# Where the exp sums are added, and who takes the relu: batch 1 and batch 0 of a fused attention and feed-forward kernel

## The chip, the cores and the metric

The kernel runs on one core of a Trainium2 chip. The metric is the device time of one execution in microseconds (us); the median of three executions counts. The profile is of one further execution. In it PE is TensorE (matmuls), PEld its weight loads, DVE VectorE, ACT ScalarE, POOL GpSimd and SP SyncE.

## What is computed

Attention with an extra term in the softmax's denominator, over 8 batches of 12 heads with 448 tokens and a head size of 64. Its output, put together to 3584 tokens of 768 columns, goes through a feed-forward layer with a squared relu:

```python
def _attn_ref(q, k, v):
    scale = 1.0 / np.sqrt(q.shape[-1])
    scores = scale * np.matmul(q, k.transpose(0, 1, 3, 2))
    m = np.max(scores, axis=-1, keepdims=True)
    e = np.exp(scores - m)
    attn = e / (np.sum(e, axis=-1, keepdims=True) + np.exp(-m) + 1e-09)
    return np.matmul(attn, v).astype(np.float32)

def _moe_ref(x, w_in, w_out):            # x: 3584 x 768, w_in: 768 x 2048, w_out: 2048 x 768
    h = x @ w_in
    r = np.maximum(h, 0.0)
    g = r * r
    return (g @ w_out).astype(np.float32)
```

## The kernel before

The work is cut into units. A unit is a pair of heads of one batch and a range of queries. Units 0 to 5 are the six pairs of batch 0 with queries 0 to 191 (`FIRST` is 192), units 6 to 11 the same pairs with queries 192 to 447, units 12 to 17 the pairs of batch 1 with all 448 queries. From unit 18 on another loop takes three units at a time; the change doesn't touch it.

A unit goes through these steps. `scores` makes two chunks of score matmuls into PSUM tiles `sp`, and ACT takes their exp into `et` in fp16. DVE adds the exps of the four key blocks into `es` (`add_chunks`). `row_sums` adds `es` over the partitions with a matmul against ones, and ACT makes the reciprocal of the sums as Ln and Exp. `values` is the matmul with v, and `normalise` on DVE multiplies its result with the reciprocal into `xt`, the transposed input of the feed-forward layer. Between these, `transposes` brings q and k of a later unit to the layout that the scores need (PE, then a copy on DVE).

The first product of the feed-forward layer is queued in tiles of 512 columns or fewer, each of 12 matmul products (two blocks of features by six blocks of 128 rows, `DCH`), and `drain(ns)` puts some of them, by their nominal time, between the steps of a unit. A tile's last product is followed by a relu and a square on DVE. In this stretch (`COLS2`) each product is two matmuls of 64 columns of weights, side by side in the array.

Each engine has its instructions in the order in which this code makes them. Every PSUM tile of transposes, row sums and first products comes from one pool, `m_psum`, with three buffers.

```python
    m_psum = ctx.enter_context(tc.tile_pool(name="m_psum", bufs=3, space=bass.MemoryType.PSUM))
    ...
    def add_chunks(u, et, es, half, step):
        n = u[3]
        if n == S:
            e = et.rearrange("p (k x) -> p k x", k=RUN)
            if step < 2:
                nc.vector.tensor_add((es, half[:, 0:2 * S])[step], e[:, 2 * step], e[:, 2 * step + 1])
            else:
                nc.vector.tensor_add(es, es, half[:, 0:2 * S])
    ...
    def row_sums(us, sums):
        ...
        zp = mp_tile()
        ...                                   # matmuls of es with ones into zp
        nc.scalar.activation(out=rcp[:, 0:m], in_=zp[:, 0:m], func=AF.Ln, bias=one_b)
        nc.scalar.activation(out=rcp[:, 0:m], in_=rcp[:, 0:m], func=AF.Exp, scale=-1.0)
    ...
    def relu_squared(hp, t0, n, f0, per):
        m = per * n
        rt = r_pool.tile([128, 512], FP16, name="rt")
        nc.vector.tensor_scalar(out=rt[:, 0:m], in0=hp[:, 0:m], scalar1=0.0, scalar2=None, op0=ALU.max)
        r = rt[:, 0:m].rearrange("p (j n) -> p j n", j=per)
        nc.vector.tensor_mul(gs[:, f0:f0 + per, t0 % RING:t0 % RING + n], r, r)
```

The loop over batch 1, `share[0]` being the nominal time of first products that a unit takes in:

```python
    for i in range(2 * NPAIR, 3 * NPAIR):
        ...
        scores(u, et, 0)
        for at in transpose_at.get(i, ()):
            transposes(*at)
        ...
        drain(share[0] * (1.2 if first else 0.45))
        scores(u, et, 1)
        if first:
            ...                               # values and row sums of units 10 and 11
        else:
            done = [prev]
            rcp = row_sums(done, (ess.pop(i - 1)[0:1],))
            values(prev, ets.pop(i - 1), xp)
        drain(share[0] * 0.15)
        for step in range(3):
            add_chunks(u, et, es, half, step)
            drain(share[0] * (0.15, 0.1, 0.15)[step])
        if i == 3 * NPAIR - 1:
            run(ins, len(ins))
            rcps[i] = row_sums([u], (ess.pop(i)[0:1],))
        normalise(done, xp, rcp)
```

In batch 0 the first products start in unit 7. Their first two tiles (features 0 to 511, from the first two of the eight pieces in which `w_in` is loaded) are made early, that is from the pairs that are done: rows of pairs 0 to 3 first, those of pairs 4 and 5 later. At the end of units 1, 3 and 5 a matmul on zeros or two keep TensorE busy (`keep_warm`).

Of the kernel before, what the change touches and what calls it, by code (L numbers as in the profile page):

```python
# [9 lines left out]
FP16 = mybir.dt.float16  # L10
AF = mybir.ActivationFunctionType
ALU = mybir.AluOpType
# [3 lines left out]
def kernel(  # L16
# [9 lines left out]
    nc = tc.nc  # L26

    B, H, S, D = q.shape
    NT, DM = out.shape
    DF = moe_w_in.shape[1]  # L30
    NPAIR = H // 2
    DCH = DM // 128
    NFFB = DF // 128
    RUN = 4
    P = S // RUN
# [17 lines left out]
    z_pool = ctx.enter_context(tc.tile_pool(name="z", bufs=3))  # L53
    r_pool = ctx.enter_context(tc.tile_pool(name="r", bufs=2))
    osb_pool = ctx.enter_context(tc.tile_pool(name="osb", bufs=2))

    s_psum = ctx.enter_context(tc.tile_pool(name="s_psum", bufs=2, space=bass.MemoryType.PSUM))
    x_psum = ctx.enter_context(tc.tile_pool(name="x_psum", bufs=1, space=bass.MemoryType.PSUM))
# [149 lines left out]

    def add_chunks(u, et, es, half, step):
        n = u[3]  # L210
        if n == S:
            e = et.rearrange("p (k x) -> p k x", k=RUN)
            if step < 2:
                nc.vector.tensor_add((es, half[:, 0:2 * S])[step], e[:, 2 * step], e[:, 2 * step + 1])  # L214
            else:
                nc.vector.tensor_add(es, es, half[:, 0:2 * S])  # L216
        elif step == 1:
            nc.vector.tensor_add(half[:, 0:4 * n], et[:, 0:4 * n], et[:, 4 * n:8 * n])
        elif step == 2:
            f = half[:, 0:4 * n].rearrange("p (h j n) -> p h j n", h=2, j=2)  # L220
            nc.vector.tensor_add(es[:, 0:2 * n].rearrange("p (h n) -> p h n", h=2), f[:, :, 0, :], f[:, :, 1, :])
# [48 lines left out]
    def mp_tile(dtype=FP32):  # L270
        if joined[0] >= 0:
            joined[0] += 1
        pool, name = (x_psum, "xp") if joined[0] > 0 and joined[0] % 4 == 0 else (m_psum, "mp")
        return pool.tile([128, 512] if dtype == FP32 else [128, 2, 512], dtype, name=name)
# [2 lines left out]

    FULL, COLS2, ROWS2 = range(3)
    mode = [FULL]
    ots = {}  # L280

    def product(out_, lhsT, rhs, start, stop):
# [7 lines left out]
    def relu_squared(hp, t0, n, f0, per):  # L290
        m = per * n
        rt = r_pool.tile([128, 512], FP16, name="rt")
        nc.vector.tensor_scalar(out=rt[:, 0:m], in0=hp[:, 0:m], scalar1=0.0, scalar2=None, op0=ALU.max)  # L293
        r = rt[:, 0:m].rearrange("p (j n) -> p j n", j=per)
        nc.vector.tensor_mul(gs[:, f0:f0 + per, t0 % RING:t0 % RING + n], r, r)  # L295

# [11 lines left out]
        relu_squared(hp, t0, n, f0, per)  # L308
        yield n / 2.4

    def tiles_in_early(n, f0, per, ready):

        xt = xts[0]
        m = per * n
        hps = [mp_tile(), mp_tile()]
        for t, dcs in ((0, range(ready)), (1, range(ready)), (0, range(ready, DCH)), (1, range(ready, DCH))):
            for j in range(per):
                fb = f0 + per * t + j
                for dc in dcs:
                    product(hps[t][:, j * n:(j + 1) * n], win[:, dc, fb * 128:(fb + 1) * 128],  # L320
                            xt[:, dc, 0:n], start=(dc == 0 and j == 0), stop=(dc == DCH - 1 and j == per - 1))
                    if dc < DCH - 1 or j < per - 1:
                        yield n / 2.4
            if dcs[-1] == DCH - 1:
                relu_squared(hps[t], 0, n, f0 + per * t, per)
                yield n / 2.4
# [68 lines left out]
    ins, outs = [], []  # L395
    groups = [0]

    def queue(t0, n):

        per = max(1, 512 // n)  # L400
        first = 0
        if t0 + n == FIRST:
            first = 2 * per
            ns = first * DCH * n / 2.4
            ins.append([ns, ns, tiles_in_early(n, 0, per, DCH - 2)])
        for f0 in range(first, NFFB, per):
            ns = per * DCH * n / 2.4
            ins.append([ns, ns, tile_in(t0, n, f0, per)])
# [10 lines left out]
    def left():  # L419
        return sum(t[0] for t in ins)  # L420

    def one(tiles):

        got = next(tiles[0][2])
        tiles[0][0] -= got
        if tiles[0][0] < 1.0:
            tiles.pop(0)
        return got

    def drain(ns):  # L430
        while ins and ns > 0:
            ns -= one(ins)

    def run(tiles, n=1):
        for _ in range(min(n, len(tiles))):
            for _ in tiles.pop(0)[2]:
                pass

    FIRST = 192
# [9 lines left out]
    def keep_warm(n):  # L449
        wp = m_psum.tile([128, 512], FP32, name="mp")  # L450
        for _ in range(n):
            nc.tensor.matmul(wp, warm[:, 0:128], warm, start=True, stop=True)

    share = [0.0]
    ets, ess, rcps = {}, {}, {}
# [27 lines left out]
    def values_of(at, xp):  # L483
        values(units[at], ets.pop(at), xp, at % 2 * units[at][3])
# [9 lines left out]
    for i in range(NPAIR):  # L494
        u, et, es, half = begin(i)
        mode[0] = COLS2
        scores(u, et, 0)
        if i < 2:
            scores(u, et, 1)
        if i in (3, 5):  # L500
            rcp = sums_of(i - 3)
        for at in transpose_at.get(i, ()):
            transposes(*at)
        if i == 0:
            cast(0, 2)
            keep_warm(1)
        if i:
            sums(i - 1)
        if i > 1:
            scores(u, et, 1)  # L510
        if i in (2, 4):
            xp = x_psum.tile([128, 512], FP32, name="xp")
        if i in (2, 3, 4):
            values_of(i - 2, xp)
        if i == 4:
            values_of(3, xp)
        if i in (3, 5):
            normalise(units[i - 3:i - 1], xp, rcp)
        if i in (1, 3, 5):
            keep_warm(1 + i // 5)  # L520


    for i in range(NPAIR, 2 * NPAIR):
        u, et, es, half = begin(i)
        two = units[i - 2:i] if i % 2 == 0 else None
        if i % 2 or i == NPAIR:
            xp = x_psum.tile([128, 512], FP32, name="xp")
        mode[0] = COLS2
        scores(u, et, 0)
        if i == NPAIR:  # L530
            sums(i - 1)
            values_of(i - 2, xp)
            values_of(i - 1, xp)
            rcp = sums_of(i - 2)
            normalise(two, xp, rcp)
            scores(u, et, 1)
            queue(0, FIRST)
            share[0] = left() / (NPAIR + 4)
        else:
            for at in transpose_at.get(i, ()):  # L540
                transposes(*at)
            drain(16 * FIRST / 2.4 if i == NPAIR + 1 else share[0] * 0.45)
            scores(u, et, 1)
            values_of(i - 1, xp)
            if two:
                rcp = sums_of(i - 2)
            drain(share[0] * 0.3)
        add_chunks(u, et, es, half, 1)
        if two and i > NPAIR:
            normalise(two, xp, rcp)  # L550
        add_chunks(u, et, es, half, 2)
        if i > NPAIR:
            drain(share[0] * 0.25)
        if i == NPAIR + 5:
            load_natural(2, 0, 3)
            for n0 in (0, HALF):
                for j in range(2):
                    load_wout(n0, j, 2)


    for i in range(2 * NPAIR, 3 * NPAIR):
        u, et, es, half = begin(i)
        prev = units[i - 1]
        first = i == 2 * NPAIR
        if not first:
            xp = x_psum.tile([128, 512], FP32, name="xp")
        mode[0] = COLS2
        scores(u, et, 0)
        for at in transpose_at.get(i, ()):
            transposes(*at)  # L570
        if i == 2 * NPAIR + 3:
            load_natural(2, 3, 6)
            load_v(2, 0, 6)
            stage(3)
# [3 lines that stand above are left out]
            done = units[i - 2:i]  # L578
            values(prev, ets.pop(i - 1), xp, prev[3])
            rcp = row_sums(done, (ess.pop(i - 2)[0:1], ess.pop(i - 1)[0:1]))  # L580
        else:
            done = [prev]
            rcp = row_sums(done, (ess.pop(i - 1)[0:1],))
            values(prev, ets.pop(i - 1), xp)
        drain(share[0] * 0.15)
        for step in range(3):
            add_chunks(u, et, es, half, step)
            drain(share[0] * (0.15, 0.1, 0.15)[step])
        if i == 3 * NPAIR - 1:
            run(ins, len(ins))  # L590
            rcps[i] = row_sums([u], (ess.pop(i)[0:1],))
        normalise(done, xp, rcp)
        if first:
            queue(FIRST, S - FIRST)
            share[0] = left() / (NPAIR - 0.2)
# [103 lines left out]
```

The softmax here doesn't subtract the row's maximum and nothing guards it: scores larger than these inputs give would overflow.

## Time and profile before

| | |
|---|---|
| median of three executions | 412.69 us (412.59 to 413.04) |
| profiled execution | 412.49 us, span of the instructions 410.6 us |
| granted TensorE clock | 0.999 |
| stretch of the changed code | about 17 to 69 us |
| one add of 112x896 fp16 | 0.62 us |
| one exp of 112x896 | 0.915 us |

A profile's page gives busy times over the whole span; since the kernel goes through stages with different limits, the busy times by stretch and the timeline of the stretch that is changed say more. In the timeline a row is an instruction or several of a kind: the start, the length, the engine, the line of the kernel, the tiles it writes and reads, their shape, and in brackets how long the engine had been idle before and what ended that. In the list of waits a row has the waiting engine and line, what it waited for, then the total, how many times, and the longest. Lines that matter here: L189 and L201 are scores, L169 exp, L214, L216, L218 and L221 the adds, L236 values, L250 row sums, L253 and L254 Ln and Exp of the reciprocal, L262 and L265 normalise, L158 transposes, L164 their copy, L286 the first product in this mode, L293 the relu, L295 the square, L352 the second product, L452 the warm matmuls.

### The profile page before, as it was taken

The numbers are of one execution on the slowest core, as the hardware profiler recorded it, in microseconds if no ns is written. First come the engines' busy times: TensorE is split into PE (matmuls) and PEld (weight loads), VectorE is DVE, ScalarE is ACT, GpSimd is POOL, SyncE is SP. The second block draws the span as 40 slices with busy tenths as digits, with TensorE's granted clock in tenths as the row PEclk, the third lists the DMA queues.
The fourth block names the chain that finished last, engine by engine and source line by source line (L and its number), as shares of the span: only waits on it lengthen the run. The fifth ranks groups of instructions, "written<-read, shape, count | busy, mean of one in ns | idle before, by whom it ended". The sixth has DMA issues, their size and how long they took to land.

```text
span 410.6 us, 10685 instructions
## 1 busy us (share of the span) xinstructions
PE 401.0 (98%) x4715; PEld 259.0 (63%) x4715; DVE 289.8 (71%) x554; ACT 234.4 (57%) x312; POOL 36.3 (9%) x58
## 2 busy tenths in 40 slices
PE   7899998999999999999999999999999999999997
PEld 3577676755576666666566666667566665555664
DVE  3778896978976787777876788867876789186000
ACT  5998997667393745559383755739464663100111
POOL 7524030020000200001000030001000000000000
PEclk9999999999999999999999999999999999999999
DMA  9999999689114891499304992297102010010222
GB/s 203 197 198 197 203 202 219 127 132 219 60 42 107 135 219 25 98 183 182 100 2 114 168 179 64 77 188 124 41 2 69 11 41 2 38 40 0 78 77 78
DMA packets 75823, 45.58 MB, mean 111 GB/s; under 512 B 42560, under 2 KB 72000, under 8 KB 75456
## 3 DMA queue, kind: packets, MB, share of 16 engines
q0 software_dynamic: 28848, 22.16, 35.6%
q1 hardware_dynamic: 46208, 22.05, 23.1%
q8 instruction: 37, 0.61, 0.6%
q10 hardware_dynamic: 720, 0.69, 0.5%
q14 instruction: 10, 0.08, 0.1%
HBM read 45.69 MB, written 17.93 MB: 155 GB/s over the span
## 4 chain that ended last, share of the span: by engine, by line
PE 89%; ACT 4%; DVE 4%; DMA 1%; issue 1%
PE mp L286 24%; PE mp L352 17%; PE mp L288 11%; PE xp L286 8%; PE sp L201 6%; PE xp L352 5%; PE mp L236 5%; PE xp L288 3%; PE xp L236 3%; PE sp L189 3%; ACT et L169 3%; PE mp L250 2%; PE mp L158 1%; DMA et<-in_k_dram 1%; DVE qk L164 1%; ACT rcp L253 1%
## 5 line engine op out<-in xcount | busy, mean ns | idle before, releaser
L169 ACT ACTIVATE et<-sp 112x896 f16<-112x896 f32 (+2 forms) x144 | 125.2, 915 | 40.7 <-PE sp L201 30.6
L352 PE MATMUL mp<-wout,gs 64*128 64x384 f16 x896 | 115.2, 322 | 0.0
L286 PEld LDWEIGHTS <-win 128*64 128x64 f16 x1536 | 83.9, 110 | 45.6 <-issue 1.5
L286 PE MATMUL mp<-xt,win 128*64 128x448 f16 (+2 forms) x1200 | 107.0, 323 | 0.3 <-DVE qk L164 0.2
L293 DVE TENSOR_SCALAR rt<-mp 128x448 f16<-128x448 f32 (+2 forms) x96 | 59.7, 622 | 26.3 <-PE mp L286 13.8
L352 PEld LDWEIGHTS <-gs 64*128 64x128 f16 x1152 | 58.1, 94 | 21.1
L295 DVE TENSOR_TENSOR gs<-rt 128x448 f16<-128x448 f16 (+2 forms) x128 | 50.2, 392 | 4.4
L352 PE MATMUL xp<-wout,gs 64*128 64x384 f16 x256 | 53.1, 323 | 0.0
L253 ACT ACTIVATE rcp<-mp,one_b 128x448 f32<-128x448 f32 (+2 forms) x42 | 26.5, 630 | 41.9 <-PE mp L250 41.7
L361 ACT ACTIVATE ot<-mp 128x384 f32<-128x384 f32 (+1 forms) x16 | 7.6, 477 | 64.5 <-PE mp L288 48.2
L201 PE MATMUL sp<-qk 64*112 64x224 f16 x480 | 43.1, 258 | 0.0
L169 ACT ACTIVATE nn<-sp 112x896 f16<-112x896 f32 x48 | 41.7, 917 | 1.6
L201 PEld LDWEIGHTS <-qk 64*112 64x112 f16 x480 | 30.6, 128 | 14.2 <-issue 3.6
L286 PE MATMUL xp<-xt,win 128*64 128x448 f16 x336 | 36.5, 352 | 0.0
L288 PEld LDWEIGHTS <-gs 128*128 128x128 f16 x256 | 24.4, 98 | 15.1 <-issue 0.4
L236 PEld LDWEIGHTS <-vn 112*64 112x64 f16 x432 | 22.4, 109 | 15.4 <-issue 3.9
L288 PE MATMUL mp<-wout,gs 128*128 128x384 f16 (+1 forms) x192 | 30.3, 317 | 0.0
L214 DVE TENSOR_TENSOR es<-et 112x896 f16<-112x896 f16 x30 | 18.7, 623 | 15.8 <-ACT et L169 15.3
L254 ACT ACTIVATE rcp<-rcp 128x448 f32<-128x448 f32 (+2 forms) x48 | 27.7, 577 | 1.5
L189 PE MATMUL sp<-qk 64*112 64x448 f16 (+2 forms) x192 | 25.8, 320 | 1.4 <-ACT et L169 0.6
L216 DVE TENSOR_TENSOR es<-es,half 112x896 f16<-112x896 f16 x42 | 26.2, 623 | 1.0
L293 DVE TENSOR_SCALAR rt<-xp 128x448 f16<-128x448 f32 x32 | 19.9, 622 | 8.2 <-PE xp L286 6.7
(63 smaller groups left out, 340.0 us busy)
## 6 DMA issues: line engine op xcount, KB each, us to landing
vn<-in_v_dram POOLq DMA_DIRECT2D x7, 672.0 KB, 9.0
out_dram<-ot SPq DMA_DIRECT2D x9, 384.0 KB, 2.3
win<-in_moe_w_in_dram POOLq DMA_DIRECT2D x8, 384.0 KB, 14.2
wout<-in_moe_w_out_dram POOLq DMA_DIRECT2D x4, 768.0 KB, 18.0
stage_q<-in_q_dram POOLq DMA_DIRECT2D x4, 676.0 KB, 11.3
stage_k<-in_k_dram POOLq DMA_DIRECT2D x4, 676.0 KB, 14.7
out_dram<-ot SPq DMA_DIRECT2D x8, 288.0 KB, 9.0
out_dram<-ot SPq DMA_DIRECT2D x9, 192.0 KB, 2.7
```

The lines of the kernel that those rows point to most:

```text
L169: nc.scalar.activation(out=out_, in_=in_, func=AF.Exp, scale=scale)
L189: nc.tensor.matmul(sp[:, h, o:o + n], qk[r, 1, x + P * kk:x + P * kk + P], qk[r, 0, x + q0:x + q0 + n], start=True, stop=True)
L201: nc.tensor.matmul(sp[:, odd, h * (S // 2):(h + 1) * (S // 2)], qk[r, which, kx:kx + 2 * P - 1:2], qk[r, 0, x:x + S // 2], start=True, sto ...
L216: nc.vector.tensor_add(es, es, half[:, 0:2 * S])
L236: nc.tensor.matmul(xp[64 * h:64 * h + 64, o:o + n], vns[b][:, 2 * pr + h, kk, :], of_head(chunk(et, u, kk // 2, kk), u, h), start=(kk == 0 ...
L253: nc.scalar.activation(out=rcp[:, 0:m], in_=zp[:, 0:m], func=AF.Ln, bias=one_b)
L254: nc.scalar.activation(out=rcp[:, 0:m], in_=rcp[:, 0:m], func=AF.Exp, scale=-1.0)
L286: nc.tensor.matmul(out_[x:x + 64], lhsT[:, x:x + 64], rhs, start=start, stop=stop)
L288: nc.tensor.matmul(out_, lhsT, rhs, start=start, stop=stop)
L293: nc.vector.tensor_scalar(out=rt[:, 0:m], in0=hp[:, 0:m], scalar1=0.0, scalar2=None, op0=ALU.max)
L295: nc.vector.tensor_mul(gs[:, f0:f0 + per, t0 % RING:t0 % RING + n], r, r)
L352: nc.tensor.matmul(o[:, 0:w], g[x:x + 64], wout[x:x + 64, fb, n0:n0 + w], start=(fb == 0), stop=(fb == NFFB - 1))
```

## The change

In batch 1 the three adds of a unit (exps of blocks 0 and 1, of 2 and 3, and the two sums) become two: one add twice as wide, of both halves of `et` into a tile of its own, and one that adds the halves of that. They move from the unit itself to the next unit, after the first chunk of its scores. The last unit keeps the three adds, the second and third now after all that is left of the first products. In units 13, 15 and 17 one relu goes to ScalarE. Both are meant to take load and interruptions off VectorE, which the relus of the first product need in the same stretch.

In batch 0 the first two tiles of the first product start in unit 5, where the warm matmuls stood, with the rows of pairs 0 and 1 alone; rows of pairs 2 and 3, and then 4 and 5, follow in unit 7 and 8. It is meant to give TensorE useful work in place of the zeros and to leave less for later. The shares of first products that go between a unit's steps are distributed anew, odd units of batch 0 taking more of them ahead of the second scores.

```diff
     def add_chunks(u, et, es, half, step):
         n = u[3]
-        if n == S:
+        if step == 3:
+            h = wide.tile([P, RUN * S], FP16, name="wide")
+            nc.vector.tensor_add(h, et[:, 0:RUN * S], et[:, RUN * S:2 * RUN * S])
+            nc.vector.tensor_add(es, h[:, 0:2 * S], h[:, 2 * S:4 * S])
+        elif n == S:
...
     def relu_squared(hp, t0, n, f0, per):
         m = per * n
         rt = r_pool.tile([128, 512], FP16, name="rt")
-        nc.vector.tensor_scalar(out=rt[:, 0:m], in0=hp[:, 0:m], scalar1=0.0, scalar2=None, op0=ALU.max)
+        if relus[0]:
+            relus[0] -= 1
+            nc.scalar.activation(out=rt[:, 0:m], in_=hp[:, 0:m], func=AF.Relu)
+        else:
+            nc.vector.tensor_scalar(out=rt[:, 0:m], in0=hp[:, 0:m], scalar1=0.0, scalar2=None, op0=ALU.max)
...
-    def tiles_in_early(n, f0, per, ready):
+    def tiles_in_early(n, f0, per):
...
-        for t, dcs in ((0, range(ready)), (1, range(ready)), (0, range(ready, DCH)), (1, range(ready, DCH))):
+        steps = (range(0, 2), range(2, DCH - 2), range(DCH - 2, DCH))
+        for t, dcs in [(t, dcs) for dcs in steps for t in range(2)]:
...
-        if i in (1, 3, 5):
-            keep_warm(1 + i // 5)
+        if i in (1, 3):
+            keep_warm(1)
+        if i == 5:
+            queue(0, FIRST)
+            drain(8 * FIRST / 2.4)
...                                            (units 6 to 11)
-            queue(0, FIRST)
-            share[0] = left() / (NPAIR + 4)
+            share[0] = left() / (NPAIR + 3.5)
         else:
             for at in transpose_at.get(i, ()):
                 transposes(*at)
-            drain(16 * FIRST / 2.4 if i == NPAIR + 1 else share[0] * 0.45)
+            drain(12 * FIRST / 2.4 if i == NPAIR + 1 else share[0] * (0.45 if two else 0.7))
             scores(u, et, 1)
             values_of(i - 1, xp)
+            drain(share[0] * (0.3 if two else 0.1))
             if two:
                 rcp = sums_of(i - 2)
-            drain(share[0] * 0.3)
...
-            drain(share[0] * 0.25)
+            drain(share[0] * (0.25 if two else 0.2))
...                                            (units 12 to 17)
+        final = i == 3 * NPAIR - 1
         scores(u, et, 0)
+        if not first:
+            add_chunks(prev, ets[i - 1], *ess[i - 1], 3)
...
-        drain(share[0] * 0.15)
-        for step in range(3):
-            add_chunks(u, et, es, half, step)
-            drain(share[0] * (0.15, 0.1, 0.15)[step])
-        if i == 3 * NPAIR - 1:
+        relus[0] = int(i in (13, 15, 17))
+        drain(share[0] * 0.3)
+        if final:
+            add_chunks(u, et, es, half, 0)
+        drain(share[0] * 0.25)
+        relus[0] = 0
+        if final:
             run(ins, len(ins))
+            add_chunks(u, et, es, half, 1)
+            add_chunks(u, et, es, half, 2)
             rcps[i] = row_sums([u], (ess.pop(i)[0:1],))
         normalise(done, xp, rcp)
```

## The prediction

> **What bounds the kernel now.** I read the page first, then busy time by stretch, then TensorE's waits between 17 and 69 us, where all the changed code runs, and last the timelines of that stretch.
>
> The page's busy line:
>
> ```profile
> PE 401.0 (98%) x4715; PEld 259.0 (63%) x4715; DVE 289.8 (71%) x554; ACT 234.4 (57%) x312; POOL 36.3 (9%) x58
> ```
>
> The busy times by stretch (stretch and its length, then busy us of PE, PEld, DVE, ACT and POOL with the number of instructions in brackets, clock, DMA):
>
> ```profile
> 17.00:36.00 19.00, 17.16 (x304) 12.73 (x304) 14.27 (x30) 17.03 (x22) 5.98 (x8) 1.00 1.45 197
> 36.00:45.00 9.00, 8.40 (x136) 5.96 (x134) 8.12 (x18) 8.63 (x12) 3.19 (x4) 1.00 1.44 199
> 45.00:60.00 15.00, 14.79 (x230) 10.78 (x226) 13.67 (x26) 13.48 (x19) 3.51 (x5) 1.00 1.32 204
> 60.00:70.00 10.00, 8.54 (x128) 6.07 (x128) 7.55 (x14) 7.18 (x11) 0.00 (x0) 1.00 1.37 219
> ```
>
> After 70 us TensorE (PE) is busy to within some 1%, so whatever the first 70 us lose or gain moves the end one for one. Within them no engine has room: from 45 to 60 us PE is at 99%, VectorE (DVE) at 91%, ScalarE (ACT) at 90%. TensorE's waits from 17 to 69 us (total us, times, longest):
>
> ```profile
> PE xp L236 <- DVE xt L265: 1.3, 2, 0.9
> PE mp L250 <- DVE es L216: 1.1, 1, 1.1
> PE sp L189 <- ACT et L169: 0.6, 2, 0.4
> PE mp L286 <- DVE qk L164: 0.2, 1, 0.2
> PE mp L250 <- DVE qk L164: 0.2, 1, 0.2
> ```
>
> They and four small ones give under 4 us: the most a perfect change could return is 1%. The timeline around the sums of unit 14 (start, length, then what):
>
> ```profile
> 50.38 0.62 DVE L214 TENSOR_TENSOR half<-et 112x896 f16<-112x896 f16 x1
> 51.03 0.62 DVE L216 TENSOR_TENSOR es<-es,half 112x896 f16<-112x896 f16 x1
> 51.58 0.62 DVE L262 TENSOR_TENSOR xt<-xp,rcp 128x448 f16<-128x448 f32 x1
> 52.11 0.61 DVE L164 COPY qk<-mp 128x896 f16<-128x896 f16 x1
> 52.78 0.38 PE L250 MATMUL mp<-es,ones 112*64 112x448 f16 x2 [0.20 <-DVE qk L164]
> ```
>
> Two things are to be seen. DVE works in program order: adds of unit 14, normalise of 13, copy of the new transposes. And PE's row sums, which need a PSUM buffer of the pool "mp" (three), waited not for their input `es`, ready at 51.65, but for that copy: they got the buffer which the transposes had used. The pool reuses the buffer freed longest ago, and this explains the other such waits too.
>
> [...] an add of 1024 columns took 0.69 us, of 512 columns 0.42, so 0.53 ns a column and 0.15 us fixed. [...]
>
> **The change part by part.**
>
> *Adds.* Of a unit's three adds (starts 0.54, 0.65 and 0.55 us apart, 1.74 together) the first two become one of 1792 columns, by the slope 0.15 + 1792 x 0.53 ns = 1.10 us, and 0.55 follows: 1.67. DVE saves 0.07 us a unit: nothing. What counts is the new place. Before, unit 14's adds ran as soon as its exps ended. Now they stand at the start of unit 15, *behind* the normalise of unit 13, which needs the reciprocal (ACT, Ln and Exp) that comes after unit 14's exps. And the copy of the transposes, for whose buffer the row sums wait, stands behind the adds. From the end of a unit's exps the chain is: Ln and Exp 1.14, normalise 0.59, adds 1.13 + 0.55, copy 0.62, semaphore 0.05: 4.1 us. The row sums of unit 15, at 57.59 today, would come 4.1 us after 54.14 (end of its exps), at 58.2: late by 0.6 even when nothing else is late.
>
> *Relus on ACT.* By the column counts a relu of 128x512 costs ACT about what its Ln of 512 columns costs, 0.69 us; DVE saves 0.71 in three units. But it queues behind the unit's Ln and Exp, and the square, still on DVE, stands before the normalise, so DVE now waits for ACT just there: about 1 us more in the chain above.
>
> *Unit by unit.* I count products per slice of the code (share now about 1945 ns) and step from one unit's row sums to the next with the measured lengths. Before, these stood at 42.88, 47.69, 52.78, 57.59, 63.19 and 67.21 us (units 12 to 17).
> - Unit 12: reciprocal 40.9, normalise to 41.5, adds to 43.2, copy to 43.8: 43.9, late by 1.0.
> - Unit 13: relu on ACT to 46.0, square, normalise 46.4, adds 46.9 to 48.6, copy to 49.2: 49.25, late by 1.55.
> - Unit 14: values 0.97 and 6 products 0.65 after the row sums, relu and square 1.06, normalise 0.55, adds 1.65, copy 0.65: 5.6 us on, 54.85, late by 2.1.
> - Unit 15: relu on ACT after 10 products, 57.0 to 57.65, square, normalise, adds: 60.4, late by 2.8 (the buffer here is the relu's, not the copy's).
> - Unit 16: the relu behind 2 products, normalise 62.7, adds from 63.25, two copies from 64.9; the tile of first products needs the buffer of the first copy, so PE stops at 63.8 until 65.55, and unit 16's second scores come behind that: 66.85, late by 3.65.
> - Unit 17: here the second and third add are put after all remaining products, so behind ACT's relu (69.45 to 70.1), a square, the first add, the last relu (from 71.05) and its square: adds from 72.1, row sums at 73.4 instead of 67.21. Even without earlier delay this order costs over 1 us: today the last relu comes after the adds.
>
> Sum: 1.0 + 0.55 + 0.5 + 0.7 + 0.85 + 2.55 = 6.2 us.
>
> *Batch 0.* Eight first products replace two warm matmuls of 0.54 us. They need `win`'s pieces 0 and 1 (columns up to 511). GpSimd's queue shows when those land, for its later loads wait for them (timeline, 17 to 21 us):
>
> ```profile
> 17.30 0.82 POOL L105 DMA_DIRECT2D win<-in_moe_w_in_dram  x1 [1.85 <-DMA win<-in_moe_w_in_dram]
> ...
> 18.98 0.85 PE L236 MATMUL xp<-et,vn 112*64 112x192 f16 x16 [0.86 <-DVE xt L265]
> ...
> 19.30 0.82 POOL L105 DMA_DIRECT2D win<-in_moe_w_in_dram  x1 [1.18 <-DMA win<-in_moe_w_in_dram]
> ...
> 20.39 0.58 ACT L253 ACTIVATE rcp<-mp,one_b 128x384 f32<-128x384 f32 x1 [0.43 <-PE mp L250]
> ```
>
> The records of landings put piece 0 at 17.02 and piece 1 at 19.02 us, just ahead of these two issues. So four of the eight products hold PE from 17.5 to 19.05 with unit 6's scores behind them: these come at 19.45 instead of 17.70, the row sums end at about 20.9 instead of 20.35, and ACT, which is gapless from 20.39 to 29.6, starts 0.5 late. What is gained is the later distribution: 3 instead of 6 products after the values of units 9 and 11, eight products fewer to do. From 29.6 us on, where ACT has gaps (0.47, 0.26, 0.63), I find unit 12's scores 0.5 us earlier. Net 0.
>
> Total: 412.7 + 6.2 = 418.9. Of such a chain some slack is usually overlooked, so 418.4.
>
> **Rivals.**
> 1. *DVE relief wins.* DVE loses 3 x 0.71 + 5 x 0.07 = 2.5 us of work, the gaps at 52.78, 61.68 and 67.21 close, and the early products take the wait at 18.98: 409.5. For it: DVE is gapless from 49 to 64 us. Against: its work is not the matter but its order, and PE is dense there anyway.
> 2. *Only the end counts.* If the row sums get another buffer than the copy's, or the adds slip in ahead of the reciprocal's wait, units 12 to 16 keep their 4.8 us and only unit 17's late adds (1.2 to 2.5) stay: 414 to 415. Against: the wait at 52.78.
> 3. *`win` decides.* If the weights land later than in this execution, all of it moves with them, since PE stops in order: up to 2 us on top, 420.5.
>
> **Range and chances.** The sign rests on two separate orders (adds behind the normalise, last adds behind the last relu), so slower is far more likely than faster; the size is a sum of six delays, each good to about 0.4 us, errors mostly in one direction. Range 414.0 to 420.8. Over 2% would be above 420.9: 0.13. Over 2% faster would be below 404.4, more than all waits give: 0.02.
>
> **What would show it.** Right: DVE idles at the squares of units 13 and 15 for ACT's relu and at the normalises for the reciprocal; the largest PE waits are row sums for DVE's copy (units 12 to 14), then for `es`; from 45 to 62 us a unit takes 5.3 to 6 us; row sums of unit 17 near 73; PE waits near 17.5 us for `win`'s landing; wide adds of 1.1 us. Wrong: row sums keep 4.8 us per unit, or DVE's wide add starts right at the end of the exps.

## The result: 422.63 us, 2.4% slower

The changed kernel takes 422.63 us in the median of four runs (421.25 to 423.43), the kernel before 412.72 on the same chip: a ratio of 1.0236, 95% interval 1.0208 to 1.0263. The direction was predicted, the size was not: 9.9 us lost instead of 5.7.

The busy line of the page after (span 421.6 us; 410.6 before) hardly differs from that of before. TensorE shows 4.6 us more, the others 2.4 at most:

```profile
PE 405.6 (96%) x4713; PEld 259.5 (62%) x4713; DVE 287.6 (68%) x546; ACT 236.8 (56%) x315; POOL 36.5 (9%) x58
```

The busy times by stretch of the kernel after, with the columns as before; the one behind POOL is the granted TensorE clock:

```profile
17.00:36.00 19.00, 16.51 (x278) 12.49 (x277) 13.21 (x28) 16.41 (x21) 4.89 (x6) 0.91 1.45 197
36.00:45.00 9.00, 7.90 (x124) 5.61 (x123) 5.60 (x11) 7.55 (x10) 4.29 (x6) 1.00 1.44 199
45.00:60.00 15.00, 12.83 (x192) 9.61 (x192) 10.81 (x20) 12.72 (x19) 3.52 (x5) 1.00 1.32 204
60.00:80.00 20.00, 14.66 (x199) 9.86 (x197) 12.21 (x22) 12.34 (x17) 0.00 (x0) 0.87 0.81 136
```

Two things are to be seen. From 45 to 60 us the three busy engines do less in the same time: TensorE 12.83 us against 14.79, VectorE 10.81 against 13.67, ScalarE 12.72 against 13.48. Nothing became the bound; they wait for each other. And the clock stands at 0.91 and 0.87 in two stretches where it was 1.00 before. TensorE's waits from 17 to 80 us:

```profile
PE mp L256 <- DVE es L222: 3.5, 1, 3.5
PE mp L293 <- DVE qk L166: 2.3, 2, 1.2
PE mp L256 <- DVE qk L166: 2.2, 3, 0.9
PE mp L293 <- DMA win<-in_moe_w_in_dram: 1.3, 1, 1.3
PE mp L256 <- DVE es L216: 0.6, 1, 0.6
```

(L256 is now the row sums, L293 the first product, L166 the copy of the transposes, L216 and L222 the adds.) The waits of before add up to under 4 us, these to over 10. The timeline around the row sums of units 14 and 15, in order of start, shows how they arise:

```profile
57.06 0.38 PE L256 MATMUL mp<-es,ones 112*64 112x448 f16 x2 [0.88 <-DVE qk L166]
...
58.31 0.58 ACT L260 ACTIVATE rcp<-rcp 128x448 f32<-128x448 f32 x1
59.33 0.60 ACT L302 ACTIVATE rt<-mp 128x512 f16<-128x512 f32 x1 [0.44 <-PE mp L293]
...
59.96 0.42 DVE L306 TENSOR_TENSOR gs<-rt 128x512 f16<-128x512 f16 x1 [1.89 <-ACT rt L302]
...
60.30 0.62 DVE L268 TENSOR_TENSOR xt<-xp,rcp 128x448 f16<-128x448 f32 x1
60.84 1.08 DVE L215 TENSOR_TENSOR wide<-et 112x1792 f16<-112x1792 f16 x1
...
61.96 0.62 DVE L216 TENSOR_TENSOR es<-wide 112x896 f16<-112x896 f16 x1
62.50 0.62 DVE L166 COPY qk<-mp 128x896 f16<-128x896 f16 x1
62.63 0.38 PE L256 MATMUL mp<-es,ones 112*64 112x448 f16 x2 [0.64 <-DVE es L216]
```

VectorE stands idle for 1.89 us in front of a square whose relu is on ScalarE. The relu itself waited for TensorE's product, as its bracket says (0.44 us), and not for Ln and Exp, which had ended by 58.89 us. Behind the square, in program order, come the normalise, the wide add (1.08 us) and the second add, and TensorE's row sums wait for the last. At the end of batch 1:

```profile
72.54 0.43 DVE L306 TENSOR_TENSOR gs<-rt 128x512 f16<-128x512 f16 x1 [3.05 <-ACT rt L302]
72.89 0.62 DVE L220 TENSOR_TENSOR es<-et 112x896 f16<-112x896 f16 x1
73.42 0.68 DVE L304 TENSOR_SCALAR rt<-mp 128x512 f16<-128x512 f32 x1
74.14 0.42 DVE L306 TENSOR_TENSOR gs<-rt 128x512 f16<-128x512 f16 x1
74.48 0.62 DVE L220 TENSOR_TENSOR half<-et 112x896 f16<-112x896 f16 x1
75.14 0.62 DVE L222 TENSOR_TENSOR es<-es,half 112x896 f16<-112x896 f16 x1
...
75.81 0.58 PE L256 MATMUL mp<-es,ones 112*64 112x448 f16 x2 [3.46 <-DVE es L222]
...
76.74 1.81 PE L364 MATMUL mp<-wout,gs 64*128 64x384 f16 x10
```

The last row: ten matmuls of the second product take 1.81 us. Before, ten took 1.03:

```profile
67.75 1.03 PE L352 MATMUL mp<-wout,gs 64*128 64x384 f16 x10
```

TensorE runs at half its clock behind this wait of 3.46 us (the windows at the end of this document show 0.50 from 74.71 us on).

The row sums of units 12 to 17 serve as time marks of batch 1. Their starts in the timelines, in us, and what follows the last to the end of the span:

| kernel | unit 12 | 13 | 14 | 15 | 16 | 17 | from there to the end |
|---|---|---|---|---|---|---|---|
| before | 42.88 | 47.69 | 52.78 | 57.59 | 63.19 | 67.21 | 343.4 |
| predicted | 43.9 | 49.25 | 54.85 | 60.4 | 66.85 | 73.4 | 343.4 |
| after | 46.10 | 51.31 | 57.06 | 62.63 | 69.25 | 75.81 | 345.8 |

From unit 12 to 17 the prediction has 29.5 us and the chip took 29.7, against 24.3 before. The two places where it failed are ahead of unit 12 (2.2 us more than predicted) and behind unit 17 (2.4 us more).

### The profile page after: what moved, and what is told of

It is laid out like the page before. It is cut to its first block, busy times and chain, and to the rows that moved or that the text cites. A ratio compares the mean times of both kernels' runs of the same rounds, so it can differ in the third digit from the quotient of the medians.

```text
span 421.6 us, 10673 instructions
## 1 busy us (share of the span) xinstructions
PE 405.6 (96%) x4713; PEld 259.5 (62%) x4713; DVE 287.6 (68%) x546; ACT 236.8 (56%) x315; POOL 36.5 (9%) x58
## 4 chain that ended last, share of the span: by engine, by line
PE 86%; DVE 5%; ACT 3%; DMA 3%; POOL 1%; issue 1%; POOLq 0%
PE mp L293 23%; PE mp L364 18%; PE mp L295 10%; PE xp L293 8%; PE sp L203 6%; PE mp L242 5%; PE xp L364 5%; PE xp L295 3%; PE xp L242 3%; DMA win<-in_moe_w_in_dram 3%; PE sp L191 2%; PE mp L256 2%; ACT et L171 1%; DVE wide L215 1%; ACT rcp L259 1%
## 5 line engine op out<-in xcount | busy, mean ns | idle before, releaser
L364 PE MATMUL mp<-wout,gs 64*128 64x384 f16 x896 | 117.0, 328 | 0.0
L293 PEld LDWEIGHTS <-win 128*64 128x64 f16 x1536 | 84.4, 110 | 49.1 <-issue 3.5
L293 PE MATMUL mp<-xt,win 128*64 128x448 f16 (+2 forms) x1200 | 108.3, 324 | 3.7 <-DVE qk L166 2.3
L304 DVE TENSOR_SCALAR rt<-mp 128x448 f16<-128x448 f32 (+2 forms) x93 | 57.8, 621 | 26.2 <-PE mp L293 13.6
L364 PEld LDWEIGHTS <-gs 64*128 64x128 f16 x1152 | 56.5, 95 | 24.4 <-issue 1.9
L293 PE MATMUL xp<-xt,win 128*64 128x448 f16 x336 | 36.4, 352 | 0.0
L220 DVE TENSOR_TENSOR es<-et 112x896 f16<-112x896 f16 x25 | 15.6, 623 | 17.6 <-ACT et L171 17.2
L222 DVE TENSOR_TENSOR es<-es,half 112x896 f16<-112x896 f16 x37 | 23.1, 623 | 0.9
```

The costliest lines, as they stand in the source:

```text
L293: nc.tensor.matmul(out_[x:x + 64], lhsT[:, x:x + 64], rhs, start=start, stop=stop)
L364: nc.tensor.matmul(o[:, 0:w], g[x:x + 64], wout[x:x + 64, fb, n0:n0 + w], start=(fb == 0), stop=(fb == NFFB - 1))
```

## The experiments

The theory after comparing the two traces had three parts: VectorE's order in batch 1, a loss in batch 0 of some 2 us that I had put at zero, and the clock behind the waits (0.50 for 6.83 us from 74.71 us on, in the trace of after). Every median stands beside that of the kernel before on the same chips, 412.55 to 412.61 us.

**Batch 1 alone, batch 0 alone.** The first kernel has batch 0 as before (`keep_warm` in unit 5, products from unit 7 on, old shares), the second batch 1 as before (three adds in the unit, no relu on ScalarE).

> Only the batch 1 part (wide adds in the next unit, relus on ScalarE, late adds of unit 17); batch 0 as before. Theory (order on VectorE plus half clock after unit 17's wait): row sums of unit 12 about 1 us later than the 42.88 us of before, 29 to 30 us from there to those of unit 17 instead of 24.3, then a clock window or two at half: 419.5 to 421. Rival (batch 0 and its wait for the weights is the main cause): 414 to 416.

> Only the batch 0 part (early tiles in unit 5, new shares); batch 1 as before. Theory: first products wait for the second piece of the weights until 19.2 us, first scores of unit 12 about 2 us later than the 35.87 us of before, and batch 1 hands that on: 414 to 415. Rival 1 (batch 1 alone costs, batch 0 is harmless): 412.7. Rival 2 (batch 0 is the main cause): 418 or more.

Batch 1 alone: 420.98 us, ratio 1.0202 (1.0187 to 1.0218). Row sums of unit 12 at 43.47, of unit 17 at 73.23, then 345.8 to the end. Batch 0 alone: 415.14, ratio 1.0062 (1.0047 to 1.0077), with nothing lost behind unit 17. Batch 1 costs 8.4 us and batch 0 2.5. Batch 1's own row sums are those of the prediction within 0.5 us (unit 12: 43.47 for 43.9; unit 17: 73.23 for 73.4). Batch 0 alone has the row sums of unit 12 at 43.86, 1.0 us late, and loses another 1.1 us in unit 16 (6.69 us for 5.60), where a tile of first products stands ahead of the second scores and waits for the buffer of the copy:

```profile
64.21 0.95 PE L293 MATMUL mp<-xt,win 128*64 128x256 f16 x14 [1.30 <-DVE qk L166]
```

In batch 1 alone the same place has a wait of 1.23 us, and unit 16 takes 6.61. Either part is enough for this loss, which fits that the two losses (8.4 and 2.5) add up to more than the 9.9 of the changed kernel.

**Relus back on VectorE**, all else as changed.

```diff
-        relus[0] = int(i in (13, 15, 17))
+        relus[0] = 0
```

> The changed kernel with all relus on VectorE. Theory: the deferred adds still stand behind the normalise; only the waits of the squares for ScalarE go (about 1 us in units 13, 15 and 17): 419.5 to 420.5. Rival (the relu on ScalarE is the cause): 415 to 417.

421.18 us, ratio 1.0207 (1.0192 to 1.0222): 1.45 us better than the changed kernel, less than expected. Part of that is the clock: executions at the same granted clock differ by 0.5 to 1.1 us (at 0.996, 420.53 and 420.78 for 421.25; at 0.992, 421.58 and 421.79 for 422.61 and 422.66). Between the row sums, unit 17 gained 0.7 us (5.84 for 6.56) and unit 15 nothing (5.67 for 5.57); unit 13 took 6.43 us for 5.21, with a stretch of half clock from 45.1 to 48.5 us in it. The relu is not the main cause.

**One relu each moved to ScalarE in the kernel before.**

> The kernel before with one relu of each of the units 13, 15 and 17 on ScalarE and nothing else (unit 13 has no tile that ends in these slices, so two relus move). Theory (the square waits for ScalarE's Ln and Exp and holds up the adds behind it): row sums of unit 15 and of unit 17 about 1 us later each: 413.8 to 415. Rival (VectorE's relief wins): 411.5 to 412.3.

413.80 us, ratio 1.0035 (1.0022 to 1.0048). Taking these relus off VectorE gained nothing; here is unit 17 (timeline), which took 4.97 us instead of 4.02:

```profile
66.22 0.58 ACT L296 ACTIVATE rt<-mp 128x512 f16<-128x512 f32 x1
66.83 0.43 DVE L300 TENSOR_TENSOR gs<-rt 128x512 f16<-128x512 f16 x1 [2.74 <-ACT rt L296]
67.17 0.62 DVE L214 TENSOR_TENSOR half<-et 112x896 f16<-112x896 f16 x1
67.83 0.62 DVE L216 TENSOR_TENSOR es<-es,half 112x896 f16<-112x896 f16 x1
...
68.50 0.38 PE L250 MATMUL mp<-es,ones 112*64 112x448 f16 x2 [2.08 <-DVE es L216]
```

ScalarE's relu is short (0.58 us), but it comes after Ln and Exp, and the square holds up the last two adds, whose exps were done at 65.2. In unit 15 it cost 0.17 us only, not the 1 us expected.

**Adds back into the unit**, still as a wide add and a second one, between the two slices of first products.

```diff
-        if not first:
-            add_chunks(prev, ets[i - 1], *ess[i - 1], 3)
...
         if final:
             add_chunks(u, et, es, half, 0)
+        else:
+            add_chunks(u, et, es, half, 3)
         drain(share[0] * 0.25)
```

> The changed kernel with the wide add and its second add in the unit itself, between the two slices of first products, instead of the next unit; all else as changed. Theory: row sums come 4.8 to 5.1 us apart again, unit 12 to 16 lose little; the late adds of unit 17 and batch 0 remain: 416 to 418. Rival (the relu on ScalarE or the width of the add is the cause): 420 to 423.

419.95 us, ratio 1.0177 (1.0160 to 1.0193): a miss for the theory as I had worded it. The row sums of units 12 to 17 stand 5.92, 5.76, 4.85, 6.62 and 6.57 us apart (changed kernel: 5.21, 5.75, 5.57, 6.62, 6.56). Unit 15 gained and, against the row sums ahead of it, unit 12; unit 13 lost 0.7. In VectorE's timeline the adds are now ahead of the normalise, but in unit 13 VectorE stands idle for 2.23 us in front of a square that waits for ScalarE's relu, and the adds are behind it:

```profile
46.60 0.36 DVE L306 TENSOR_TENSOR gs<-rt 128x384 f16<-128x384 f16 x1 [2.23 <-ACT rt L302]
46.87 1.08 DVE L215 TENSOR_TENSOR wide<-et 112x1792 f16<-112x1792 f16 x1
47.99 0.62 DVE L216 TENSOR_TENSOR es<-wide 112x896 f16<-112x896 f16 x1
48.53 0.62 DVE L268 TENSOR_TENSOR xt<-xp,rcp 128x448 f16<-128x448 f32 x1
49.07 0.61 DVE L166 COPY qk<-mp 128x896 f16<-128x896 f16 x1
```

From the row sums of units 10 and 11 to those of unit 17 this kernel needs 33.9 us, the changed one 34.9. So the place in the next unit costs 1.0 us there; the rest of the 2.7 us between the medians goes with the clock (all four executions at 0.996, those of the changed kernel at 0.988 to 0.996). What stays, by the timeline, is that all the adds of a unit stand behind a relu and square that wait for products made after the row sums. The row sums of one unit, products, relu, square, both adds, normalise, copy and the row sums of the next unit then form a ring, and swapping adds and normalise in it changes little. Before, the first add at least ran ahead of that relu.

**Unit 17's adds first**, ahead of the last relus, in the changed kernel.

```diff
+        if final:
+            add_chunks(u, et, es, half, 0)
+            add_chunks(u, et, es, half, 1)
+            add_chunks(u, et, es, half, 2)
         relus[0] = int(i in (13, 15, 17))
         drain(share[0] * 0.3)
-        if final:
-            add_chunks(u, et, es, half, 0)
         drain(share[0] * 0.25)
         relus[0] = 0
         if final:
             run(ins, len(ins))
-            add_chunks(u, et, es, half, 1)
-            add_chunks(u, et, es, half, 2)
```

> The changed kernel with all three adds of unit 17 ahead of its last relus, right behind unit 16's values. Theory (the late adds make TensorE idle 3.46 us, and that idle halves the clock for 6.8 us after it): row sums of unit 17 come 3.3 to 3.6 us after those of unit 16 instead of 6.57, no half clock after them, 416.5 to 418. Rival (the half clock comes of all the gaps before, or of something else than the idle time): only the 3 us, 419.5 to 420.

417.70 us (416.71 to 418.20), ratio 1.0115 (1.0098 to 1.0131): 4.9 us of the 9.9 come back. The row sums of unit 17 follow those of unit 16 by 3.02 us (6.57 changed, 4.02 before). The tail, from there to the end, is 343.8 us, with no half clock behind unit 17 (this profile, at a granted clock of 0.996, has a stretch at 0.51 in batch 1, from 46.0 to 49.4 us), and the place of the adds is all that was altered.

**TensorE kept busy in that wait**: 14 matmuls on zeros ahead of unit 17's row sums, nothing else.

```diff
             add_chunks(u, et, es, half, 2)
+            keep_warm(14)
             rcps[i] = row_sums([u], (ess.pop(i)[0:1],))
```

> The changed kernel with 14 warm matmuls (zeros, 14 times 0.21 us) in the wait of unit 17's row sums, nothing else. Theory: the row sums still come about 6.6 us after those of unit 16, but the clock stays full after them; from there to the end 343.4 to 343.8 us instead of 345.8: 420.2 to 421. Rival (the 2.4 us lost behind the wait are another wait, of ScalarE or of buffers): no change, 422.6.

(The 0.21 us agree with the trace of before, where one such matmul takes 0.39 us and two take 0.60.) 419.99 us in the median (419.38 to 423.62), ratio 1.0197 (1.0160 to 1.0233). The row sums still come 6.57 us after those of unit 16, but the tail is 343.4 us as before, and ten matmuls of the second product take 0.98 us:

```profile
71.28 3.19 PE L464 MATMUL mp<-warm 128*128 128x512 f16 x14
74.81 0.38 PE L256 MATMUL mp<-es,ones 112*64 112x448 f16 x2 [0.34 <-DVE es L222]
75.12 0.40 PE L191 MATMUL sp<-qk 64*112 64x448 f16 x2
75.35 0.98 PE L364 MATMUL mp<-wout,gs 64*128 64x384 f16 x10
```

The granted clock from 75.12 to 78.53 us is 1.00. The 2.4 us behind the wait are thus the clock. Useless work of 3 us made the kernel 2.6 us faster. Three runs were at a granted clock of 1.0; the fourth, 423.62, at 0.992. Where its half clock lay was not recorded.

**Batch 0's two suspects undone together**, with batch 1 as before: in unit 5 just the four products of the first tile (`drain(4 * FIRST / 2.4)`, whose weights have landed), and the shares 0.45, 0.3 and 0.25 for odd units too.

> Only the batch 0 part, with its two suspects undone: in unit 5 just the four early products of the first tile (first piece of the weights), and the old shares in odd units. Theory: no wait for the second piece and none of 1.2 us for the copy in front of unit 11's second scores: 412.3 to 413.2. Rival (starting early costs by itself, by buffers that are held longer): 414.5 to 415.2 as with the whole batch 0 part.

414.69 us, ratio 1.0050 (1.0037 to 1.0064): a miss. The wait for the weights was gone, but not the one in unit 11 (timeline of TensorE):

```profile
34.12 0.25 PE L293 MATMUL mp<-xt,win 128*64 128x192 f16 x2
35.81 0.52 PE L293 MATMUL mp<-xt,win 128*64 128x192 f16 x8 [1.44 <-DVE qk L166]
36.26 0.42 PE L191 MATMUL sp<-qk 64*112 64x256 f16 x4
```

A new tile of first products begins ahead of unit 11's second scores, needs the PSUM buffer that VectorE's copy must first empty, and TensorE holds the scores back with it. Batch 0 alone has the same with 1.11 us. It is the tiles' borders that count: in the kernel before a tile ends exactly at the end of that slice and the next begins behind scores and values, when the copy is done:

```profile
33.67 0.58 PE L286 MATMUL mp<-xt,win 128*64 128x192 f16 x10
34.18 0.42 PE L189 MATMUL sp<-qk 64*112 64x256 f16 x4
34.54 0.63 PE L236 MATMUL xp<-et,vn 112*64 112x256 f16 x8
35.25 0.69 PE L286 MATMUL mp<-xt,win 128*64 128x192 f16 x12
```

By the code, 16 products were made up to the end of unit 7's first slice there; here they are 20 (4 and 16), as in batch 0 alone (8 and 12), and the shares differ too (775 and 741 ns for 768). This shifts the border.

**The same early start, with the borders kept**: the kernel before with four early products, and the later shares such that each slice from unit 8 on holds the products of before.

```diff
-            queue(0, FIRST)
-            share[0] = left() / (NPAIR + 4)
+            share[0] = (left() + 4 * FIRST / 2.4) / (NPAIR + 4)
...
-            drain(16 * FIRST / 2.4 if i == NPAIR + 1 else share[0] * 0.45)
+            drain(12 * FIRST / 2.4 if i == NPAIR + 1 else share[0] * 0.45)
```

> The kernel before with four products of the first tile in unit 5 in place of the two warm matmuls, and the later shares set so that from unit 8 on each slice holds the same products as before. Theory (the batch 0 part loses by the place of the tiles' borders: a tile's first product that needs the buffer of unit 11's copy stands in front of the second scores): no wait of 1.2 us there, 412.2 to 412.8. Rival (the early start costs by itself): 414.5.

412.55 us, ratio 1.0000 (0.9992 to 1.0009): the loss is gone and nothing is gained. The early start of four products by itself is harmless and useless. (Unlike the kernel above, it also makes the row sums of batch 0's pairs ahead of a slice of products, as before; no run has that alone.) TensorE does four products fewer in unit 7 and waits for ScalarE instead (its waits for exp 1.1 us in place of 0.6).

**Only the width left** of the batch 1 part: no relu on ScalarE, both adds in the unit, unit 17's adds first. The batch 0 part is still in.

> The changed kernel without relus on ScalarE, with the two adds in the unit itself and unit 17's adds ahead of its last relus: of the batch 1 part only the width of the first add and one block of adds instead of three places are left. Theory (order costs, width doesn't): the loss of the batch 0 part, 2.5 us, and 0.5 to 1 us for adds in one block behind the relu: 415.2 to 416.3. Rival (the wide add itself, or the tile it needs, costs): 417.5 or more.

416.66 us, ratio 1.0098 (1.0084 to 1.0111), 0.4 us over what was expected. Against batch 0 alone it loses 1.5. The row sums: 5.08, 5.76, 4.81, 6.62, 3.02 us apart; batch 0 alone has 5.06, 5.19, 4.81, 6.69, 4.13. So unit 17 gains 1.1, unit 14 loses 0.6 (its adds in one block behind the relu). The rest lies outside batch 1: a lower clock (the profiled runs were granted 0.995 and 0.999), and 0.7 us behind unit 17, where the second product now waits for the last relu. The width itself shows no cost: from start to start 1.12 us for the wide add against 0.54 and 0.65 for the two that it replaces. No run has the wide add alone in the kernel before.

**A version that beats both.** In the kernel before, the wait of 1.1 us for unit 17's sums comes of a relu between its adds. Here the three adds come first:

```diff
+        last = i == 3 * NPAIR - 1
         for step in range(3):
             add_chunks(u, et, es, half, step)
-            drain(share[0] * (0.15, 0.1, 0.15)[step])
+            if not last:
+                drain(share[0] * (0.15, 0.1, 0.15)[step])
```

> The kernel before with all three adds of unit 17 ahead of the relus that follow unit 16's values. Theory (TensorE's wait of 1.1 us for unit 17's sums comes from a relu that stands between its adds): row sums of unit 17 about 3.0 us after those of unit 16 instead of 4.02, 411.5 to 412. Rival (what is gained there is lost in a wait for the last tiles): 412.6.

411.70 us in 11 runs, ratio 0.9979 (0.9970 to 0.9987). The row sums come 3.02 us after unit 16's instead of 4.02; 0.2 of that is lost behind them. Then with two more moves: the four early products with the borders kept, and each normalise of batch 1 behind the copy of the next unit.

> The kernel before with three moves: unit 17's adds first (0.9 us less, as run alone), four early products instead of warm matmuls, and each normalise of batch 1 behind the copy of the next unit's transposes, so that the row sums get their buffer 0.5 us earlier. Theory: the waits at 52.78 and 61.68 us go (0.4 us and less) and little more: 410.8 to 411.5. Rival (normalise later holds up the values, which need its PSUM tile): 412 or more.

411.58 us in 10 runs, ratio 0.9975 (0.9966 to 0.9984): not to be told from the one before, and just over the expected range. The row sums of unit 14 follow those of unit 13 0.27 us sooner, those of unit 15 follow 0.1 later.

## Why the prediction was right and wrong

*Adds and unit 17: right.* 6.2 us were worked out for batch 1. In the changed kernel units 12 to 17 take 29.7 us for 24.3, 5.4 more, and unit 12's adds, first behind the normalise, 1.2 (5.19 us from the row sums of units 10 and 11 instead of 4.02): 6.6. The waits are those that were named: the row sums of units 12 to 14 wait for the copy, those of 15 and 17 for `es`. The late adds of unit 17 count most (4.9 us with the clock behind them), the deferral 1.0 us between the row sums.

*Relus: the words wrong, the steps right.* "About 1 us more in the chain above" did not show in unit 15, which took 5.57 us with its relu on ScalarE and 5.67 without. There the relu waits for TensorE's product (0.44 us), and the step for unit 15 had it start after ten products, so the predicted time fits all the same. The relus of 128x512 on ScalarE took 0.58 and 0.60 us for the estimated 0.69, and the trace of after has one table load on ScalarE, at 2.2 us, none at a relu. Only in unit 17 is a cost of over 0.2 us shown (0.7 us in the changed kernel, 0.95 in the kernel before); what unit 13's relu costs, the half clock there hides.

*The clock: the step that failed.* The sum "412.7 + 6.2" takes TensorE at full clock throughout; what the clock does after a wait is no term of it, although the late adds of unit 17 leave TensorE waiting (3.46 us). The trace of after shows a clock of 0.50 for 3.41 us from 20.09 us on and for 6.83 us from 74.71 us on (last section). These two cost 1.0 us in batch 0 (row sums of units 6 and 7 at 27.33 us; in the kernel with the warm matmuls, whose batch 0 is the same and ran at full clock, at 26.31) and 2.4 us behind unit 17. Together these 3.4 us are most of the 4.8 by which the loss between the two profiled spans exceeds 6.2; without them the profiled 423.43 us would be 420.0 by this estimate, inside the predicted 414.0 to 420.8. The times of the changed kernel go with the clock: 421.25 us at a granted clock of 0.996, 422.61 and 422.66 at 0.992, 423.43 at 0.988.

*"Net 0" for batch 0: wrong as well.* The row sums of units 10 and 11 come 2.0 us late (40.91 us for 38.87). Of that, 1.0 is the clock, and 0.2 is there already ahead of the changed code (16.58 for 16.39). The wait for the weights was seen, and it cost less than the 0.5 us: in batch 0 alone the row sums of units 4 and 5 end at 20.68 us instead of 20.34, and those of units 6 and 7 start at 26.07 instead of 25.96. What failed is "I find unit 12's scores 0.5 us earlier". Seven products stand ahead of unit 11's second scores, two of them of the next tile, whose buffer waits for the copy. Measured: 1.1 us of waiting ahead of those scores, and 7.87 us from the row sums of units 8 and 9 to those of units 10 and 11 instead of 7.18, where a gain was expected.

In sum: 1.2 + 5.4 in batch 1, 2.0 ahead of it, 2.4 behind it, 11.0 us between the two profiled spans; the median, at a granted clock of 0.992, has one stretch of half clock less than the profiled run at 0.988 (my estimate: 3.41 us at half in 421 us make 0.004).

*Rivals.* "DVE relief wins" (409.5) is contradicted by the relus moved alone: +1.2 us. "Only the end counts" was half true: it is the largest part, but units 12 to 16 did lose. "`win` decides": in batch 0 alone TensorE waited 1.0 us for the weights, and 0.1 us of it was left by units 6 and 7; in the changed kernel the wait (1.3 us) stands in the stretch ahead of the first half clock. The range failed because "errors mostly in one direction" was meant for slack overlooked; the errors went the other way.

## What to carry to other kernels

On an engine that works in order, as VectorE does in these timelines, ask of each moved instruction what it now stands behind and what that waits for; busy time saved says little when the order closes a ring between engines (two relus of 0.68 us moved off VectorE made the kernel before 1.2 us slower). If a step makes TensorE wait for some microseconds, look at the clock after it: here it fell to 0.50 for 6.83 us, from the last 1.1 us of the 3.46 us of waiting on, which cost another 2.4 us. Where a pool is shared, count whose buffer a tile gets and which later instructions stand behind it (1.1 us of waiting ahead of unit 11's second scores).

## What the runs showed of the hardware

The clock fell without full idleness: to 0.50 at 20.09 us, with TensorE busy for 2.08 of the 3.41 us before. The clock records in the trace of after give stretches of 13.65, 3.41, 51.20, 6.83 and 341.33 us, all multiples of 3.41, and a last one that the end cuts; the two at half clock start 54.62 us apart, 16 times as much. So within this trace they lie on a fixed grid. Where it starts differs from run to run: half clock begins at 20.09 us here, at 45.1 with the relus back on VectorE and at 46.0 with unit 17's adds first, 7.3 and 7.6 times 3.41 us later. The four executions of the changed kernel were granted 0.988, 0.996, 0.992 and 0.992. Stretches of the changed kernel on this grid, two ahead of half clock and between them one that isn't:

```profile
16.68:20.09 3.41, 2.08 (x30) 1.19 (x32) 2.29 (x6) 2.50 (x4) 1.46 (x2) 1.00 1.46 197
20.09:23.51 3.42, 3.42 (x38) 2.80 (x40) 0.64 (x2) 2.68 (x4) 0.95 (x2) 0.50 1.45 199
...
43.99:47.40 3.41, 2.09 (x22) 1.41 (x23) 2.85 (x5) 3.22 (x5) 0.00 (x0) 1.00 1.33 206
47.40:50.82 3.42, 3.42 (x61) 2.49 (x56) 2.62 (x5) 2.52 (x5) 0.00 (x0) 1.00 1.31 205
...
71.29:74.71 3.42, 1.06 (x20) 0.79 (x16) 2.13 (x5) 1.19 (x3) 0.00 (x0) 1.00 0.27 57
74.71:78.12 3.41, 2.31 (x14) 1.03 (x16) 1.55 (x3) 1.65 (x3) 0.00 (x0) 0.50 0.00 0
```

With TensorE busy for 2.08 of 3.41 us the next stretch ran at half; with 2.09 it did not. In the kernel before with two relus moved, whose profiled run was granted 1.0, 1.88 us in 3.41 (64.54 to 67.95 us) did not halve it either, while 1.85 us in 3.40 did with all relus on VectorE (41.7 to 45.1 us, 0.50 after) and with unit 17's adds first (42.6 to 46.0 us, 0.51 after). So TensorE's busy time, as the profile models it, does not decide by itself, and what does, no run here settles.
